# Attention followed by a feed-forward block: the second product by seven half-size block products, one PSUM bank for the first

## The chip, the cores and the metric

The kernel runs on one core of one Trainium2 chip. The metric is the device time of one execution, in microseconds (us). Times given are medians of the runs shown; the profile is of one execution.

## The reference

Attention over 4 batches of 8 heads, 768 tokens, head size 64, in which a query sees the keys of its own hash bucket only; then a feed-forward block with an activation made of softplus and erf. All in float32.

```python
q_bits = (np.einsum('bhsd,dk->bhsk', q, proj) > 0)      # 6 bits; the same for k
mask = q_bucket[:, :, :, None] == k_bucket[:, :, None, :]
scores = np.where(mask, scale * np.matmul(q, k.transpose(0, 1, 3, 2)), -1000000000.0)
attn = softmax(scores)
x = (attn @ v).transpose(0, 2, 1, 3).reshape(3072, 512)
h = x @ w_in                                            # 512 -> 2048
sp = np.maximum(h, 0.0) + np.log1p(np.exp(-np.abs(h)))
out = (h * erf(sp)) @ w_out                             # 2048 -> 512
```

## The kernel before, in words

**Attention** (`attention`) goes over 16 pairs of heads. Scores are computed with the keys on the partitions, ACT takes the exponential straight from PSUM (three slots of two banks), DVE sums the exponentials for the divisor, PE weighs v. Between these, `square_high`, `keep_normal`, `move_bits`, `mask_bits` and `add_rest` turn the weights' float64 bits into float32. The exponential is taken without subtracting a maximum. That is safe while the scores are bounded, so a bound is worked out, and a flag decides at the end whether a general version (`general`) must run too. Before the change the bound comes from the largest magnitudes of q and k: during the feed-forward block `fetch_part` loads q and k once more, 64 pieces, `extremes` takes their maxima on DVE, and `judge` makes the flag.

**The feed-forward block** (`feed_forward`) goes over 6 tiles of 512 tokens (t), each in 4 steps (c); step p = 4 t + c, called a pair in the prediction, treats four of the 16 blocks of 128 hidden features. The first product x @ w_in is done by Strassen's scheme in Winograd's form: `product` computes P1 to P7, seven products of half-size blocks in place of eight, four matmuls of 128x128x256 each. They are summed in three PSUM banks X, Y and Z. `read` (ACT) copies X to the tile h at four stages of its sum, `complete` (DVE) adds Y or Z to three of the four quarters. The sums of x blocks that the scheme needs (`presum_x`) exist twice, one set for each of two x tiles; the sums of w_in are made once in attention.

The activation works on two units of 128 x 1024 a pair: `absolute`, `exponential`, `one_more`, `lost`, `logarithm`, `softplus`, `correct`, `square`, three times `factor` (ACT) and `multiply` (DVE), `saturate`, `gate`. Exp and tanh are in one ACT table, ln in another.

The second product (`project`, L1081) is the plain one: the gated blocks are stationary, w_out streams by, 8 x 2 matmuls of 128x128x512 a pair, 384 in all. They are summed over the four steps in four PSUM banks, one for each 128 tokens; at the end of a tile `store` copies each bank and sends it.

A matmul of float32 operands shows in the trace as two rows of matmul and two of weight load.

**The order** is no order of the source. Every step of both parts is an `Op` with an engine, a cost, a rank, what it comes after, and what buffers it takes and frees. `arrange` plays these through on a model clock and emits each engine's instructions in that order, so every engine then works its list from front to back. On PE the first products rank before the second ones, and h has four buffers, so that the first products run up to four pairs ahead. `late` brings the last pair of heads to its end inside the feed-forward block.

Of the kernel before, what the change touches and what calls it, by code (L numbers as in the profile page):

```python
# [64 lines left out]
S_MAX = 4.0  # L66
# [28 lines left out]
def arrange(ops, rooms):  # L95


    ready = {op.name: None for op in ops}
    names = {op.name: op for op in ops}
    waiting = {}  # L100
    for op in sorted(ops, key=lambda op: op.rank):
        waiting.setdefault(op.engine, []).append(op)
    clock = dict.fromkeys(waiting, 0.0)
    rings = {ring: [] for ring in rooms}
    released = {}
    table = "exp"
    order = []
    while len(order) < len(ops):
        best = None
        for engine, queue in waiting.items():  # L110
            for op in queue:
                start = clock[engine]
                needs = [a for a in op.after if a in names]
                if any(ready[a] is None for a in needs):
                    continue
                for a in needs:
                    away = 0.0 if names[a].engine == engine else names[a].late
                    start = max(start, ready[a] + away)
                if op.take:
                    ring = rings[op.take[0]]  # L120
                    if len(ring) >= rooms[op.take[0]]:
                        end = released.get(ring[-rooms[op.take[0]]])
                        if end is None:
                            continue
                        start = max(start, end)
                if best is None or (start, engine != best[1], op.rank) < (
                    best[0],
                    False,
                    best[2].rank,
                ):  # L130
                    best = start, engine, op
        start, engine, op = best
# [4 lines left out]
        clock[engine] = ready[op.name] = end  # L137
# [4 lines left out]
        waiting[engine].remove(op)  # L142
        order.append(op)
    return order
# [3 lines left out]
def kernel(  # L148
# [34 lines left out]
    norm = ctx.enter_context(tc.tile_pool(name="norm", bufs=1))  # L183
# [14 lines left out]
    most = const.tile([P, 2, B * H], F32, name="most")  # L198
# [58 lines left out]

    def load_x(t):

        x, _ = blocks[t % 2]  # L260
        n = t * T
        while n < (t + 1) * T:
            b, n0 = divmod(n, S)
            m = min(S - n0, (t + 1) * T - n)
            nc.sync.dma_start(
                out=x[:, :, n - t * T : n - t * T + m],
                in_=xs[b][:, :, n0 : n0 + m].rearrange("k p t -> p k t"),
            )
            n += m

    def presum_x(t, k):

        x, ts = blocks[t % 2]
        b11, b12, b21, b22 = x[:, 0:2, 0:TH], x[:, 0:2, TH:T], x[:, 2:4, 0:TH], x[:, 2:4, TH:T]
        t1, t2, t4 = (ts[:, n, :, :] for n in range(3))
        out_, one_, two_ = ((t1, b12, b11), (t2, b22, t1), (b12, b22, b12), (t4, b21, t2))[k]
        nc.vector.tensor_tensor(out=out_, in0=one_, in1=two_, op=ALU.subtract)

    def block_tiles(pool, n):
        x = pool.tile([P, NK, T], F32, name=f"x{n}")  # L280
        ts = pool.tile([P, 3, 2, TH], F32, name=f"ts{n}")
        return x, ts

    blocks.append(block_tiles(const, 0))


# [72 lines left out]
    def attention():  # L359
        NS = NPAIR * 4  # L360
        with (
# [165 lines left out]
            def home(i):  # L527
                return xst if i < NPAIR - 1 else norm
# [14 lines left out]
            def keep_divisor(h):  # L543
                i, half = divmod(h, 2)
                d = pairs[i]
                if half == 0:
                    d["z"] = home(i).tile([P, S], F32, name="z", tag="z")
                nc.scalar.copy(out=d["z"][:, half * HS : (half + 1) * HS], in_=d.pop("z_ps"))

            def leave(h):  # L550
# [4 lines left out]
                if half == 0:  # L555
                    d["x"] = home(i).tile([P, S], F32, name="x", tag="x")
# [44 lines left out]
            def widen(i):  # L601
                d = pairs[i]
                rd = d.pop("rd")
                d["r"] = home(i).tile([P, S], F32, name="r", tag="z")
# [139 lines left out]
            for i in range(NPAIR):  # L744
                n = 4 * i
                if i:
# [6 lines left out]
                        (("weigh", n - 9), ("bits_of", i - 1)),  # L753
# [12 lines left out]
                    )  # L766
                if i == NPAIR - 1:
# [42 lines left out]
            for k in range(4):  # L810
                op(presum_x, (0, k), "DVE", 0.62, (2, 31, 8 + k), (("load_x", 0), ("presum_x", 0, k - 1)))
# [116 lines left out]

    def feed_forward(check, late):
        with (  # L930
            tc.tile_pool(name="xb", bufs=1) as xb,
            tc.tile_pool(name="hp", bufs=4) as hp,
            tc.tile_pool(name="sp", bufs=4) as sp,
            tc.tile_pool(name="work", bufs=2) as work,
            tc.tile_pool(name="outp", bufs=2) as outp,
# [4 lines left out]
            del blocks[1:]  # L940
            blocks.append(block_tiles(xb, 1))
            st = {}

            def product(p, name):
# [3 lines left out]
                x, ts = blocks[t % 2]  # L948
                b11, t3 = x[:, 0:2, 0:TH], x[:, 0:2, TH:T]
                b21, b22 = x[:, 2:4, 0:TH], x[:, 2:4, TH:T]  # L950
                t1, t2, t4 = (ts[:, n, :, :] for n in range(3))
# [3 lines left out]
                into, a, b, first, last = dict(  # L955
                    P1=("X", a11, b11, True, False),
                    P2=("Y", a12, b21, True, True),
                    P3=("Z", s4, b22, False, True),
                    P4=("X", a22, t4, False, True),
                    P5=("Z", s1, t1, True, False),  # L960
                    P6=("X", s2, t2, False, False),
                    P7=("X", s3, t3, False, False),
                )[name]
                if first:
                    tag = into if p != 1 else f"o{'XYZ'.index(into)}"
                    d[into] = ps_f.tile([P, 2, TH], F32, name=into, tag=tag)
                for u in range(2):
                    f = (2 * c + u) * P
                    for kc in range(2):
                        nc.tensor.matmul(  # L970
                            out=d[into][:, u, :],
# [7 lines left out]
            def read(p, q):  # L979

                d = st[p]
                if "h" not in d:
                    d["h"] = hp.tile([P, 2, 4, TH], F32, name="h", tag="h")
                nc.scalar.copy(out=d["h"][:, :, q, :], in_=d["X"])  # L984

            def complete(p, q, which):
                d = st[p]
                h = d["h"][:, :, q, :]
                nc.vector.tensor_tensor(out=h, in0=d[which], in1=h, op=ALU.add)

            def unit(p, u):
                return st[p]["h"][:, u, :, :].rearrange("p q t -> p (q t)")

            def absolute(p, u):
                e = st[p]["e", u] = work.tile([P, 2 * T], F32, name="e", tag="e")
                nc.vector.tensor_scalar(  # L996
                    out=e[:, :].bitcast(I32),
                    in0=unit(p, u).bitcast(I32),
                    scalar1=0x7FFFFFFF,
                    scalar2=None,  # L1000
                    op0=ALU.bitwise_and,
                )

            def exponential(p, u):
                e = st[p]["e", u]
                nc.scalar.activation(out=e, in_=e, func=AF.Exp, scale=-1.0)  # L1006

            def one_more(p, u):
                w = st[p]["w", u] = work.tile([P, 2 * T], F32, name="w", tag="wq", bufs=4)
                nc.scalar.activation(out=w, in_=st[p]["e", u], func=AF.Identity, bias=1.0)  # L1010

            def lost(p, u):

                w = st[p]["w", u]
                nc.vector.scalar_tensor_tensor(  # L1015
                    out=w, in0=w, scalar=-1.0, in1=st[p]["e", u], op0=ALU.add, op1=ALU.subtract
                )

            def logarithm(p, u):
                s = st[p]["s", u] = sp.tile([P, 2 * T], F32, name="s", tag="s")  # L1020
                nc.scalar.activation(out=s, in_=st[p].pop(("e", u)), func=AF.Ln, bias=1.0)  # L1021

            def softplus(p, u):
                s = st[p]["s", u]
                nc.vector.scalar_tensor_tensor(  # L1025
                    out=s, in0=unit(p, u), scalar=0.0, in1=s, op0=ALU.max, op1=ALU.add
                )

            def correct(p, u):
                s = st[p]["s", u]  # L1030
                nc.vector.scalar_tensor_tensor(  # L1031
                    out=s,
                    in0=s,
                    scalar=S_MAX,
                    in1=st[p].pop(("w", u)),
                    op0=ALU.min,
                    op1=ALU.subtract,
                )

            def square(p, u):  # L1040
                z = st[p]["z", u] = work.tile([P, 2 * T], F32, name="z", tag="z")
                nc.scalar.activation(out=z, in_=st[p]["s", u], func=AF.Square)  # L1042

            def factor(p, u, j):
                z = st[p]["z", u]
                if j == 2:
                    q = z
                else:
                    q = work.tile([P, 2 * T], F32, name="q", tag="wq", bufs=4)
                st[p]["q", u, j] = q  # L1050
                nc.scalar.activation(out=q, in_=z, func=AF.Square, bias=cq[:, j : j + 1])  # L1051

            def multiply(p, u, j):
                s = st[p]["s", u]
                nc.vector.scalar_tensor_tensor(  # L1055
                    out=s,
# [364 lines left out]
```

## Time and profile before

| | |
|---|---|
| median of 3 runs | 979.61 us (976.65 to 980.2) |
| the profiled execution | 979.03 us |
| its span, first to last instruction | 976.7 us |
| busy: PE, DVE, ACT | 960.0, 836.3, 733.3 us |
| mean granted PE clock | 1.000 |
| first products of the feed-forward block begin | 345.5 us |
| matmul rows of L1081, of attention's scores (f32) | 768, 768 |

Busy time is the time in which an engine had an instruction in work. Matmuls overlap in the pipeline, so the mean duration of a row is longer than the distance between two rows. Attention fills about the first third of the span, the feed-forward block the rest.

### The profile page before, as it was taken

How to read it: one execution, taken by the hardware profiler on the slowest of the kernel's cores; microseconds unless marked ns; L12 is line 12 of the kernel's file. 1: busy time of each engine (PE TensorE's matmuls, PEld its weight loads, DVE VectorE, ACT ScalarE, POOL GpSimd, SP SyncE). 2: the span in 40 equal slices, each digit the busy share in tenths (PEclk: the TensorE clock that was granted, in tenths of full speed). 3: DMA queues.
4: the chain of work that ended last, by engine and by line, in shares of the span. 5: the costliest groups of instructions: out<-in, count | busy, mean ns of one | idle time of the engine just before them, and what ended most of it. 6: DMA issues, size and time to landing. Idle time of an engine off the chain costs nothing.

```text
span 976.7 us, 11534 instructions
## 1 busy us (share of the span) xinstructions
PE 960.0 (98%) x4297; PEld 559.0 (57%) x4297; DVE 836.3 (86%) x1074; ACT 733.3 (75%) x866; POOL 18.0 (2%) x37
## 2 busy tenths in 40 slices
PE   8999999999999999999999999999999999999997
PEld 3454444444444477666665666666666666666543
DVE  4999998999999928989999999988988899888861
ACT  4775776676676629789889888988698889987970
POOL 0000000000000000000000000000000000000000
PEclk9999999999999999999999999999999999999999
DMA  8455555665455122210121002210220000000001
GB/s 189 114 147 139 135 140 163 151 171 147 127 154 149 56 79 79 92 33 17 54 97 33 32 28 86 71 33 27 65 91 17 1 31 13 1 1 21 23 1 46
DMA packets 61888, 74.55 MB, mean 76 GB/s; under 512 B 33888, under 2 KB 44640, under 8 KB 61824
## 3 DMA queue, kind: packets, MB, share of 16 engines
q1 hardware_dynamic: 56880, 56.75, 21.2%
q0 software_dynamic: 4640, 16.78, 5.5%
q8 instruction: 36, 0.59, 0.3%
q10 hardware_dynamic: 304, 0.20, 0.1%
q14 instruction: 28, 0.23, 0.1%
HBM read 60.92 MB, written 12.78 MB: 75 GB/s over the span
## 4 chain that ended last, share of the span: by engine, by line
PE 92%; DVE 4%; ACT 2%; DMA 1%; issue 0%; SPq 0%; DVEq 0%; ACTq 0%
PE o_ps L1081 32%; PE X L970 16%; PE st L479 15%; PE av L519 12%; PE Z L970 8%; PE Y L970 4%; PE z_ps L536 2%; PE bits L316 2%; DVE s L1055 1%; DMA q<-in_qkT_dram 1%; DVE sum L505 1%; ACT e L493 1%; DVE s L1031 0%; DVE s L1025 0%; DVE most L1109 0%
## 5 line engine op out<-in xcount | busy, mean ns | idle before, releaser
L1081 PE MATMUL o_ps<-w_out_sb,h 128*128 128x512 f32 x768 | 341.4, 592 | 0.0
L1081 PEld LDWEIGHTS o_ps<-w_out_sb,h 128*128 128x128 f32 x768 | 145.8, 190 | 153.0 <-issue 148.0
L493 ACT ACTIVATE e<-st 128x768 f32<-128x768 f32 x192 | 148.9, 818 | 12.7 <-PE st L479 12.6
L479 PE MATMUL st<-q,k 64*128 64x384 f32 x768 | 156.1, 484 | 0.0
L519 PE MATMUL av<-e,v 128*64 128x385 f32 (+1 forms) x768 | 129.5, 486 | 0.0
L505 DVE TENSOR_TENSOR sum<-sum,e 128x768 f32<-128x768 f32 x128 | 121.7, 951 | 7.6 <-ACT e L493 0.7
L1055 DVE SCALAR_TENSOR_TENSOR s<-q,s 128x1024 f32<-128x1024 f32 x96 | 116.3, 1220 | 8.6 <-ACT q L1051 5.5
L1051 ACT ACTIVATE q<-z,cq 128x1024 f32<-128x1024 f32 x96 | 105.8, 1142 | 1.4
L519 PEld LDWEIGHTS av<-e,v 128*64 128x64 f32 x768 | 56.0, 137 | 68.0 <-issue 65.4
L970 PE MATMUL X<-x,w_in_sb 128*128 128x256 f32 x384 | 90.6, 380 | 2.1 <-ACT h L984 1.6
L479 PEld LDWEIGHTS st<-q,k 64*128 64x128 f32 x768 | 68.5, 188 | 33.5 <-issue 33.3
L970 PEld LDWEIGHTS X<-x,w_in_sb 128*128 128x128 f32 x384 | 72.8, 190 | 25.4 <-issue 12.1
L984 ACT COPY h<-X 128x512 f32<-128x512 f32 x96 | 55.2, 575 | 41.7 <-PE X L970 35.6
L557 ACT COPY x<-av 128x384 f32<-128x384 f32 x32 | 15.3, 478 | 92.7 <-PE av L519 74.7
L1015 DVE SCALAR_TENSOR_TENSOR w<-w,e 128x1024 f32<-128x1024 f32 x48 | 58.3, 1221 | 17.7 <-ACT w L1010 17.5
L1025 DVE SCALAR_TENSOR_TENSOR s<-h,s 128x1024 f32<-128x1024 f32 x48 | 58.5, 1220 | 17.1 <-ACT s L1021 17.1
L1042 ACT ACTIVATE z<-s 128x1024 f32<-128x1024 f32 x48 | 50.5, 1052 | 29.0 <-DVE s L1031 28.8
L479 PE MATMUL st<-qb,kb 64*128 64x384 bf16 x384 | 63.8, 325 | 4.1 <-ACT e L493 3.2
L1070 DVE TENSOR_TENSOR h<-h,s 128x1024 f32<-128x1024 f32 x48 | 57.1, 1216 | 3.2 <-ACT s L1066 3.2
L1031 DVE SCALAR_TENSOR_TENSOR s<-s,w 128x1024 f32<-128x1024 f32 x48 | 58.6, 1222 | 1.2
L1006 ACT ACTIVATE e<-e 128x1024 f32<-128x1024 f32 x48 | 50.4, 1050 | 10.6 <-DVE e L996 10.5
L1055 DVE SCALAR_TENSOR_TENSOR s<-z,s 128x1024 f32<-128x1024 f32 x48 | 57.1, 1216 | 0.0
(82 smaller groups left out, 1244.2 us busy)
## 6 DMA issues: line engine op xcount, KB each, us to landing
t<-in_qkT_dram SPq DMA_DIRECT2D x64, 192.0 KB
raw<-in_w_in_dram POOLq DMA_DIRECT2D x16, 512.0 KB, 3.9
raw<-in_w_out_dram POOLq DMA_DIRECT2D x16, 512.0 KB, 3.7
v<-in_v_dram SPq DMA_DIRECT2D x32, 192.0 KB
r<-rd SPq DMA_DIRECT2D x32, 192.0 KB
xs<-x SPq DMA_DIRECT2D x16, 384.0 KB
out_dram<-ob SPq DMA_DIRECT2D x24, 256.0 KB
q<-in_qkT_dram SPq DMA_DIRECT2D x30, 192.0 KB
```

Of the source, the lines that this page charges most:

```text
L479: nc.tensor.matmul(out=st[:, ab, 0:HS], lhsT=d["k" + src][rows, keys], rhs=d["q" + src][rows, cols], start=(part == 0), stop=(part == 1),)
L493: nc.scalar.activation(out=e[:, :, 0:HS], in_=st[:, :, 0:HS], func=AF.Exp, scale=scale)
L505: nc.vector.tensor_tensor(out=d[key], in0=before, in1=block(n, c)[:, :, 0:HS], op=ALU.add)
L519: nc.tensor.matmul(out=d["av"][rows, 0:w], lhsT=d["v"][:, g * GC + c, rows], rhs=e[:, ab, 0:w], start=(g == 0 and c == 0), stop=(g == 1 an ...
L970: nc.tensor.matmul(out=d[into][:, u, :], lhsT=a[:, kc, f : f + P], rhs=b[:, kc, :], start=(first and u == 0 and kc == 0), stop=(last and u ...
L1015: nc.vector.scalar_tensor_tensor(out=w, in0=w, scalar=-1.0, in1=st[p]["e", u], op0=ALU.add, op1=ALU.subtract)
L1025: nc.vector.scalar_tensor_tensor(out=s, in0=unit(p, u), scalar=0.0, in1=s, op0=ALU.max, op1=ALU.add)
L1031: nc.vector.scalar_tensor_tensor(out=s, in0=s, scalar=S_MAX, in1=st[p].pop(("w", u)), op0=ALU.min, op1=ALU.subtract,)
L1051: nc.scalar.activation(out=q, in_=z, func=AF.Square, bias=cq[:, j : j + 1])
L1055: nc.vector.scalar_tensor_tensor(out=s, in0=st[p].pop(("q", u, j)), scalar=ERF_Q[j][1], in1=s, op0=ALU.add, op1=ALU.mult,)
L1070: nc.vector.tensor_tensor(out=h, in0=h, in1=st[p].pop(("s", u)), op=ALU.mult)
L1081: nc.tensor.matmul(out=o_live[tt], lhsT=st[p]["h"][:, u, 2 * fh + half, sub * P : (sub + 1) * P], rhs=w_out_sb[:, fh * NF // 2 + 2 * c + u ...
```

## The change

- **Second product.** The plain product becomes the same seven-product scheme, M1 to M7, on blocks of the gated activations and of w_out, 28 matmuls of 128x128x256 a pair. Each M has a PSUM bank of its own, summed over the four steps of a tile. Sums of gated blocks (`presum_g`, 4 a pair, DVE); sums of w_out (`presum_w`, once for each c, DVE), kept in DRAM (`keep_w`) and loaded again for each later pair (`load_w`, 768 KB, ring of two). At a tile's end `combine` adds the seven banks up, one ACT copy and seven DVE additions, and sends four quarters.
- **First product.** The seven M banks and one bank X are all eight. X takes every first product after the third pair, evicted seven times a pair (4 `read`, 3 `complete`). The first three pairs borrow M banks.
- **Activation.** softplus(h) is computed as ln(1 + exp(min(h, 3.98))) with its correction: `absolute` becomes `clip`, `softplus` is left out. h is held in halves of tokens (8 buffers), e has 4 buffers, w 6.
- **Bound.** `measure` sums the squares of q and k on ACT during attention (64 activations with a summed output); `fetch_part` and `extremes` go. `judge` uses these sums early in the feed-forward block.
- **Buffers.** The sums of x blocks exist once (`x_sum`). The last pair of heads uses the second x tile.
- **Order.** `arrange` takes priorities for each kind of step and a patience of 0.16 us, by which a step of the first rank goes ahead of one that could start that much earlier.

```diff
+PRIORITY = dict(
+    clip=(-0.37, 0.71),
...
+    project=-7.76,
+)
+PATIENCE = 0.16
...
+            start, op = min(
+                (
+                    (start, op)
+                    for start, op in starts
+                    if start <= first + (patience if op.rank[0] == 0 and engine != "PE" else 0.0)
+                ),
+                key=lambda each: (each[1].rank, each[0]),
+            )
...
+            def measure(i, n, half):
+
+                cols = slice(half * HS, (half + 1) * HS)
+                nc.scalar.activation(
+                    out=x_sum[:, 0, :, :].rearrange("p k t -> p (k t)")[:, 0:HS],
+                    in_=pairs[i]["qk"[n]][:, cols],
+                    func=AF.Square,
+                    accum_out=stats[:, n, i, half : half + 1],
+                )
...
-                        (("weigh", n - 9), ("bits_of", i - 1)),
+                        (("weigh", n - 9), ("bits_of", i - 1))
+                        + tuple(("measure", i - 3, m, half) for m in range(2) for half in range(2)),
...
+            def clip(p, v):
+                e = st[p]["e", v] = own("e")
                 nc.vector.tensor_scalar(
+                    out=e, in0=unit(p, v), scalar1=H_MAX, scalar2=None, op0=ALU.min
+                )
...
+            def presum_g(p, k):
...
+                out_, one_, two_, op_ = (
+                    lambda: (d["S", 0], a21, a22, ALU.add),
+                    lambda: (d["S", 1], d["S", 0], a11, ALU.subtract),
+                    lambda: (a21, a11, a21, ALU.subtract),
+                    lambda: (d["S", 3], a12, d["S", 1], ALU.subtract),
+                )[k]()
+                nc.vector.tensor_tensor(out=out_, in0=one_, in1=two_, op=op_)
...
+            def load_w(p):
+                w_sums[p] = wtp.tile([P, 3, 2, TH], F32, name="wt", tag="wt")
+                nc.sync.dma_start(out=w_sums[p], in_=wt_dram[p % NC4])
...
+            def project(p, name, k):
 
                 t, c = divmod(p, NC4)
...
+                a, b = dict(
+                    M1=lambda: (d["h", 0][:, 0, :, :], w_block(c, 0, 0)),
+                    M2=lambda: (d["h", 0][:, 1, :, :], w_block(c, 1, 0)),
+                    M3=lambda: (d["S", 3], w_block(c, 1, 1)),
+                    M4=lambda: (d["h", 1][:, 1, :, :], t4),
+                    M5=lambda: (d["S", 0], t1),
+                    M6=lambda: (d["S", 1], t2),
+                    M7=lambda: (d["h", 1][:, 0, :, :], w_block(c, 0, 1)),
+                )[name]()
...
+                sub, u = divmod(k, 2)
+                nc.tensor.matmul(
+                    out=banks[name][:, sub, :],
+                    lhsT=a[:, u, sub * P : (sub + 1) * P],
+                    rhs=b[:, u, :],
+                    start=(c == 0 and k == 0),
+                    stop=(c == NC4 - 1 and k == 3),
+                    skip_group_check=True,
+                )
...
+            def combine(t, k):
+
+                if k == 0:
+                    outs["u"] = outp.tile([P, 2, TH], F32, name="u", tag="u")
+                    nc.scalar.copy(out=outs["u"], in_=banks["M1"])
                     return
...
+                nc.vector.tensor_tensor(out=outs[into], in0=banks[name], in1=one, op=ALU.add)
...
+            ORDER = ("M1", "M2", "M4", "M5", "M6", "M7", "M3")
...
+                if p < FILL:
+                    x, y, z = (("M1", "M2", "M4"), ("M5", "M6", "M7"), ("M3", "X", "X"))[p]
...
+                else:
+                    steps = (
+                        ("P1", "X", 0, read),
+                        ("P6", "X", 1, read),
+                        ("P7", "X", 3, read),
+                        ("P4", "X", 2, read),
+                        ("P2", "X", 0, complete),
+                        ("P5", "X", 3, complete),
+                        ("P3", "X", 1, complete),
+                    )
...
-            for each in arrange(ops, dict(h=4, e=2, wq=4, s=4, z=2, ob=2)):
+            for each in arrange(ops, dict(h=8, e=4, w=6, wt=2), PATIENCE):
                 each.emit()
```

In `ORDER`, M1 and M2 need the gate of the first token half, M4 that of the second, M5, M6, M7 and M3 the sums S1 to S4 made from both.

More of the change, by code (lines that the diff above doesn't have):

```diff
@@ L104, in arrange @@
+PATIENCE = 0.16
+def arrange(ops, rooms, patience=0.0):
+    names = {op.name: op for op in ops}
+    users, missing = {}, {}
+    for op in ops:
+        needs = {a for a in op.after if a in names}
+        missing[op.name] = len(needs)
+        for a in needs:
+            users.setdefault(a, []).append(op)
+    ranked = sorted(ops, key=lambda op: op.rank)
+    clock = {op.engine: 0.0 for op in ranked}
+    ready, released = {}, {}
     rings = {ring: [] for ring in rooms}
-    released = {}
+    open_ops = {engine: [] for engine in clock}
@@ L106, in arrange, with open_up, start_of @@
     table = "exp"
     order = []
+    def open_up(op):
+        at = 0.0
+        for a in op.after:
+            if a in names:
+                away = 0.0 if names[a].engine == op.engine else names[a].late
+                at = max(at, ready[a] + away)
+        open_ops[op.engine].append((op, at))
+    def start_of(op, at):
+        at = max(at, clock[op.engine])
+        if op.take:
+            ring, room = rings[op.take[0]], rooms[op.take[0]]
+            if len(ring) >= room:
+                at = max(at, released.get(ring[-room], float("inf")))
+        return at
@@ L108, in arrange @@
+    for op in ranked:
+        if not missing[op.name]:
+            open_up(op)
     while len(order) < len(ops):
         best = None
[L110 to L131, printed above, removed]
@@ L132, in arrange @@
-        start, engine, op = best
+        for engine, entries in open_ops.items():
+            starts = [(start_of(op, at), op) for op, at in entries]
+            starts = [each for each in starts if each[0] < float("inf")]
+            if not starts:
+                continue
+            first = min(start for start, _ in starts)
+            start, op = min(
[6 more added lines that the diff above has]
+            )
+            if best is None or start < best[0]:
+                best = start, op
@@ L136, in arrange @@
             end += TABLE_LOAD
-        clock[engine] = ready[op.name] = end
+        clock[op.engine] = ready[op.name] = end
         if op.take:
@@ L141, in arrange @@
             released[what] = end + op.late
-        waiting[engine].remove(op)
+        open_ops[op.engine] = [each for each in open_ops[op.engine] if each[0] is not op]
         order.append(op)
+        for user in users.get(op.name, ()):
+            missing[user.name] -= 1
+            if not missing[user.name]:
+                open_up(user)
     return order
@@ L970, in product @@
                         nc.tensor.matmul(
-                            out=d[into][:, u, :],
+                            out=d[where][:, u, :],
                             lhsT=a[:, kc, f : f + P],
@@ L977, in product, with quarter @@
                         )
-            def read(p, q):
+            def quarter(p, q):
+                fh, th = divmod(q, 2)
                 d = st[p]
[L982 to L989, printed above, removed]
@@ L1008, in one_more, with read @@
[L1008 to L1014, printed above, removed]
+                if ("h", th) not in d:
+                    d["h", th] = hp.tile([P, 2, 2, TH], F32, name="h", tag="h")
+                return d["h", th][:, fh, :, :]
+            def read(p, q, where):
+                nc.scalar.copy(out=quarter(p, q), in_=st[p][where])
@@ new lines, in first_ops @@
+                last_of, seen = {}, set()
+                for k, (name, where, q, fn) in enumerate(steps):
+                    after = (("load", t), ("presum", t, ready.get(name, -1)))
+                    if where in last_of:
+                        after += (last_of[where],)
+                    if where == "X" and chain["X"]:
+                        after += (chain["X"],)
+                    if chain["P"]:
+                        after += (chain["P"],)
+                    op(
+                        (name, p),
+                        "PE",
+                        1.73,
+                        (0, p, k),
+                        product,
+                        (p, name, where, name in ("P1", "P2", "P5"), name in ("P4", "P2", "P3")),
+                        after=after,
+                        late=0.3,
+                    )
+                    chain["P"] = (name, p)
+                    me = (fn.__name__, p, q)
+                    after = ((name, p),)
+                    if fn is complete:
+                        after += (("read", p, q),)
+                    op(
+                        me,
+                        "ACT" if fn is read else "DVE",
+                        0.58 if fn is read else 0.69,
+                        (0, p, k),
+                        fn,
+                        (p, q, where),
+                        after=after,
+                        take=("h", (p, q % 2)) if q % 2 not in seen else None,
+                    )
+                    seen.add(q % 2)
+                    last_of[where] = me
+                    if where == "X":
+                        chain["X"] = me
@@ L1296, in feed_forward @@
                     )
+                op(("check", 0), "PE", 0.3, (0, 1, 9), check, (), after=(("P3", 0), ("late", 0)), late=1.5)
+                for each in ops:
+                    if each.name == ("P2", FILL - 1):
+                        each.after += (("check", 0),)
             else:
```

672 lines of the change are left out of this document (357 added, 315 removed).

## The prediction

> **What bounds the kernel now.** I read the page's busy table first, then the windows cut where the feed-forward (FF) begins, where the last gate ends and at the end, then the chain of waits.
>
> ```profile
> PE 960.0 (98%) x4297; PEld 559.0 (57%) x4297; DVE 836.3 (86%) x1074; ACT 733.3 (75%) x866; POOL 18.0 (2%) x37
> 30.00:345.00 315.00, 310.62 (x2044) 147.00 (x2042) 291.59 (x449) 208.58 (x315) 15.55 (x29) 1.00 0.52 139
> 345.40:363.30 17.90, 17.83 (x82) 14.97 (x83) 4.06 (x7) 3.80 (x8) 0.00 (x0) 1.00 0.26 83
> 363.30:948.40 585.10, 581.65 (x1986) 376.16 (x1985) 520.63 (x563) 504.36 (x523) 0.00 (x0) 1.00 0.12 40
> 948.40:976.70 28.30, 22.87 (x54) 9.84 (x52) 2.76 (x4) 0.00 (x0) 0.00 (x0) 0.99 0.11 40
> PE 92%; DVE 4%; ACT 2%; DMA 1%; issue 0%; SPq 0%; DVEq 0%; ACTq 0%
> 363.99 5.18 PE X L970 x24
> 923.20 48.08 PE o_ps L1081 x112
> 945.95 2.36 DVE L1070 TENSOR_TENSOR h<-h,s 128x1024 f32<-128x1024 f32 x2 [0.66 <-ACT s L1066]
> 971.30 0.69 DVE L1095 COPY ob<-o_ps 128x512 f32<-128x512 f32 x1 [2.74 <-PE o_ps L1081]
> ```
>
> A window row gives start:end, its length, then busy time of PE, weight loads, DVE, ACT, POOL, granted clock. The reader should see a PE that is full in attention and FF at clock 1.00, and a chain that is 92% PE. The last gate ends at 948.3 and PE still has 23.0 us of second products to run, until 971.3 (923.20 + 48.08). DVE is 89.0% busy in the long window (520.63/585.10), ACT 86.2% (504.36/585.10): close seconds.
>
> The two chain rows give the PE's cadence, which the groups' mean durations (pipeline included) do not: a 256-column row costs 5.18/24 = 0.2158 us, a 512-column row 48.08/112 = 0.4293 us. Each f32 matmul of the program is two rows.
>
> **The change part by part.** Groups that are removed or serve as prices (busy, mean ns of one | idle before, releaser):
>
> ```profile
> L1081 PE MATMUL o_ps<-w_out_sb,h 128*128 128x512 f32 x768 | 341.4, 592 | 0.0
> L970 PEld LDWEIGHTS X<-x,w_in_sb 128*128 128x128 f32 x384 | 72.8, 190 | 25.4 <-issue 12.1 <-ACT h L984 3.0 <-ACT x L557 1.2
> L1025 DVE SCALAR_TENSOR_TENSOR s<-h,s 128x1024 f32<-128x1024 f32 x48 | 58.5, 1220 | 17.1 <-ACT s L1021 17.1
> L1109 DVE TENSOR_REDUCE most<-t 128x1 f32<-128x384 f32 x64 | 32.5, 543 | 0.0
> L1095 DVE COPY ob<-o_ps 128x512 f32<-128x512 f32 x24 | 16.5, 686 | 22.0 <-PE o_ps L1081 21.9
> L277 DVE TENSOR_TENSOR ts<-x,ts 128x512 f32<-128x512 f32 x12 | 8.2, 684 | 0.1
> L996 DVE TENSOR_SCALAR e<-h 128x1024 int32<-128x1024 int32 x48 | 31.7, 685 | 0.1
> L984 ACT COPY h<-X 128x512 f32<-128x512 f32 x96 | 55.2, 575 | 41.7 <-PE X L970 35.6 <-PE o_ps L1081 3.8 <-issue 1.7
> L1051 ACT ACTIVATE q<-z,cq 128x1024 f32<-128x1024 f32 x96 | 105.8, 1142 | 1.4
> ```
>
> *Second product on PE.* Out go 768 rows of 512 columns, 768 x 0.4293 = 329.7 us. In come 24 pairs x 7 products x 4 matmuls x 2 = 1344 rows of 256 columns. The first product already runs such rows, with a fresh 128x128 weight load (190 ns) hidden in each 215.8 ns, so 1344 x 0.2158 = 290.1 us. Saved: 39.6 us, all on the path. Half-size rows cost 1.5 us more than half of a full row would (1344 x (0.2158 - 0.4293/2)); that is included.
>
> *DVE in FF.* Out: softplus's maximum 58.5, the extremes 32.5, the stores 16.5, together 107.5. In: four sums of the gated blocks per pair, 96 x 0.684 = 65.7; sums of w_out, 16 x 0.684 = 10.9; combine, 6 tiles x 7 x 0.686 = 28.8; together 105.4. The clip replaces the absolute value, one source of the same shape, so 0.685 again. Net -2.1 us: DVE's work does not fall, while PE's falls by 39.6.
>
> *ACT in FF.* Four reads, twelve activations and the table switches a pair stay; combine adds a copy a tile, 6 x 0.575 = 3.5 us. I take the 48 table loads as unchanged; where the new order needs one more a pair, that is 24 x 1.28 = 31 us more of ACT.
>
> ```profile
> L1021 ACT ACT_TABLE_LOAD x24 | 30.8, 1283 | 0.4
> L1066 ACT ACT_TABLE_LOAD x19 | 24.4, 1283 | 0.3
> L1006 ACT ACT_TABLE_LOAD x5 | 6.4, 1283 | 0.1
> ```
>
> *Does PE stay the bound?* Moved 39.6 us earlier, PE would end at 931.7. Behind the last gate come M4, M5, M6, M7, M3: 40 rows, 8.6 us. So the last gate must end by 923.1, 559.8 us after 363.3. ACT then needs (504.4 + 3.5)/559.8 = 90.7% where 86.2% was seen. DVE: 520.6 - 2.1, less two of the four w_out sums, which fit the idle fill (5.5), and less the last sums and combine, which come after the gate (7.5), is 505.5, or 90.3% where 89.0% was seen. So two ends: PE full, cost 0; or ACT at its old density, 507.9/0.862 = 589.2, last gate at 952.5, PE's end at 952.5 + 8.6 + 0.3 = 961.4, cost 29.7. The rows that choose:
>
> ```profile
> ACT h L984 <- PE X L970: 35.6, 28, 2.9
> ACT z L1042 <- DVE s L1031: 28.8, 20, 2.2
> ACT h L984 <- PE o_ps L1081: 3.8, 5, 1.0
> DVE w L1015 <- ACT w L1010: 17.5, 24, 1.6
> ```
>
> (Waits inside FF: total, times, longest.) Of ACT's 80.7 us of idle time in the window, 39.4 are reads that wait for a full PE: ACT's old density was partly PE's pace. Without those it is 504.4/(585.1 - 39.4) = 92.4%, above what is needed. The rest is ACT and DVE waiting for each other, which more buffers in flight (four e, six w) ease and do not abolish. I stand nearer to the first end: +7.
>
> *One bank X for all seven first products after the third pair.* Each must be evicted before the next starts; PE runs second products meanwhile. PE, then ACT, from the timeline:
>
> ```profile
> 599.99 1.89 PE L970 MATMUL X<-ts,w_sum 128*128 128x256 f32 x8
> 601.72 1.88 PE L1081 MATMUL o_ps<-w_out_sb,h 128*128 128x512 f32 x4
> 603.44 1.89 PE L970 MATMUL X<-x,w_in_sb 128*128 128x256 f32 x8
> 602.09 0.57 ACT L984 COPY h<-X 128x512 f32<-128x512 f32 x1
> 624.30 0.58 ACT L984 COPY h<-X 128x512 f32<-128x512 f32 x1 [0.16 <-PE o_ps L1081]
> ```
>
> The product is over at 601.88, read from 602.09 to 602.66, and the next X product starts at 603.44: one second product, 1.72 us, covers an eviction that needs 0.21 + 0.57. After the change there are seven evictions and seven second products (12.1 us) a pair, exactly one each, with about 0.9 us over for ACT or DVE to finish the instruction they are in (1.14 or 1.22 at most, about half on average). Cost 0 while second products are at hand; if not, 0.8 to 2 us a product. The row at 624.30 shows a read held until a second product freed its h buffer: P runs four pairs ahead, and that stays.
>
> *Attention.* 64 squares on ACT. Nearest rows:
>
> ```profile
> L557 ACT COPY x<-av 128x384 f32<-128x384 f32 x32 | 15.3, 478 | 92.7 <-PE av L519 74.7 <-DMA xs<-x 11.8 <-PE st L479 3.5
> L403 ACT ACTIVATE keep<-raw 128x512 f32<-128x512 f32 x32 | 22.1, 690 | 4.1 <-DVE top L439 4.1
> PE st L479 <- ACT e L493: 3.2, 3, 1.2
> raw<-in_w_out_dram POOLq DMA_DIRECT2D x16, 512.0 KB, 3.7
> ```
>
> No row shows an activation that also sums; I bound it by 0.478 and 0.690, 31 to 44 us in all. ACT is idle for 106.4 of the 315 us, the larger part some 2.9 us at a time ahead of a `leave` (92.7/32), so they fit. If one stands in front of an exponential, scores wait for the PSUM slot: at the mean of the wait row, 1.07 us, 64 of them would cost 68 us. Ends 0 and 68; the idle row is nearer, and I take +1. Each next fetch of q, k, v now waits on SP for the squares of three pairs before; the row sums' transfers of earlier pairs stand behind it on SP, and the hash product of the next pair waits for it. It costs nothing while the squares are done a pair later.
>
> *Transfers.* 64 fetches of 192 KB leave FF. Four stores and twenty loads of 768 KB for the w_out sums come; by the 512 KB row an estimate of 5.6 us each, and each has about a pair's time (24 us) between the buffer coming free and its use at M4. Cost 0; 5 us a pair if that cover went. On SP the loads of x and the output stand behind them.
>
> *Single x sums.* At five tile borders two DVE sums (1.4 us) stand between the old P5 and the new P6, covered by P3, P1 and second products; inside the +7.
>
> *Tail and rest.* After M7 three combines (2.1 us) run beside M3 (1.7), then the last combine and its transfer, behind two others sent just before: +1, ends 0 and 2. The bound's check moves from mid-FF into the fill, where DVE is idle: 0.
>
> Sum against the profiled execution: 976.7 - 39.6 + 7 + 1 + 1 = 946.1 us of span. It took 979.03 us with 2.3 around the span, so 948.4; the median of the three runs lies 0.6 higher: 949.
>
> **The rivals.**
> 1. *The vector engines keep their pace.* ACT at 86.2%: cost 29.7 in place of 7, so 972. For it: the ACT-DVE waits above. Against it: the 39.4 us of reads waiting for PE.
> 2. *The one bank stalls PE, slower.* PE stands still at X because evictions answer late or second products are missing. 21 pairs x 7 = 147 products. If each eviction first waits for a whole instruction of 1.14 us, the gap is 0.21 + 1.14 + 0.57 + 0.26 (the restart) = 2.18 against 1.73 of cover: 0.45 x 147 = 66, from a floor of 942 to 1008. It decides from 0.29 us a product on (42/147). For it: DVE and ACT would both be near 91%. Against it: the read at 602.09, 0.2 us after its product's end. The 0.26 is the first product after a wait, 1.99 against 1.73:
>
> ```profile
> 345.47 1.99 PE X L970 x8
> 347.46 1.73 PE Y L970 x8
> ```
>
> The Trainium skill, "Perfetto Trace Analysis", section "Optimizing Tensor Performance", says that independent matmul groups should rotate through different PSUM banks so that an eviction overlaps the next group's matmuls; by it the old X, Y, Z are right and one X is a step back, and the time is this rival's. The trace bears it out only where nothing else stands ready for PE. The same section says that larger matmuls are more efficient; the two chain rows agree, with the 1.5 us above.
>
> 3. *PE gains less than counted*, because weight loads of the gated blocks show: 190 of 215.8 ns is close. If every row cost 0.245 the gain would be gone (979). Against it: the 24 rows at 363.99 with the same loads.
>
> **How the numbers follow.** Near-full PE, 938 to 960: 0.62. Pace kept, 960 to 975: 0.20. No net change, within 0.5% (what a measurement here can tell from none, 4.9 us): 0.06. Rival 2: 0.07. The squares' bad end: 0.03. Rival 3 is in the 0.06. Below 938: 0.02. The low end is the floor 976.7 - 39.6 + 1 + 1 + 2.9 = 942, less 4 of the 6 us in which PE ran no row in FF before (625.8 us from 345.5 to 971.3, against 329.7 + 290.1 of rows). The high end is rival 1. Faster 0.84, same 0.06, slower 0.10.
>
> **What would show it.** Rows of the second product 1344 at 0.216 cadence; FF's DVE busy time within 5 us of before and ACT's within 8; PE idle in FF of 5 to 12 us; the last gate some 9 to 15 us before PE's end. Rival 1 shows as PE waiting at second products for DVE with ACT-DVE waits unchanged, rival 2 as many PE waits of X for ACT and DVE reads. I am wrong if attention's end moves beyond 350, if the table loads exceed 48, or if PE's idle time in FF is above 30 us.

## The result, and the profile after

The changed kernel takes 938.06 us (median of 4 runs, 937.16 to 941.07); the kernel before, with a run added on the same chip, 979.83. The ratio is 0.9586, with a 95% interval of 0.9556 to 0.9615: 41.8 us less. The forecast was 949, with a range of 938 to 972, so the time lies at the range's lower edge: 0.06 us inside, with two of the four runs below it. The profiled execution is the slowest of the four, 941.07 us with a span of 939.2.

From the page after, the windows cut at the same places as before (attention; from 363.3 to the end of the last gate), and three rows of the chain of waits (start, length, what):

```profile
PE 921.9 (98%) x4875; PEld 666.6 (71%) x4875; DVE 835.4 (89%) x1093; ACT 779.0 (83%) x1004; POOL 18.5 (2%) x37
30.00:345.00 315.00, 312.00 (x2062) 146.32 (x2058) 294.77 (x452) 247.94 (x438) 16.37 (x30) 1.00 0.52 139
363.30:921.30 558.00, 556.00 (x2573) 487.35 (x2572) 506.77 (x564) 508.42 (x530) 0.00 (x0) 1.00 0.16 52
PE 92%; DVE 4%; DMA 2%; ACT 1%; issue 0%; SPq 0%; ACTq 0%; DVEq 0%
346.02 7.17 PE M L1044 x32
895.79 33.68 PE M L1184 x156
```

PE is as full as before (98%), at the same clock, and still 92% of the chain. A row of the second product costs 33.68/156 = 0.2159 us, the price that the first product had. ACT and DVE are now 91.1% and 90.8% busy in the long window, where they were 86.2% and 89.0%.

The ends of the feed-forward (FF), from the timeline after:

```profile
920.02 1.23 DVE L1126 TENSOR_TENSOR h<-h,e 128x1024 f32<-128x1024 f32 x1 [1.12 <-ACT e L1122]
929.29 1.89 PE L1184 MATMUL M<-w_out_sb,S 128*128 128x256 f32 x8
931.55 0.68 DVE L1213 TENSOR_TENSOR v<-M,v 128x512 f32<-128x512 f32 x1
932.26 1.58 SPq L1216 DMA_DIRECT2D out_dram<-v  x1
```

The last gate ends at 921.3, 27 us earlier than before. PE issues its last product from 929.29 to 931.0. So FF takes PE 585.0 us (346.0 to 931.0) where it took 625.8: 580.2 of the two products' rows and 4.8 beside them, against 619.8 and 6.0. The span's 37.5 us less are 39.6 of rows and 1.2 of gaps, less 0.55 in attention and 2.8 at the end (931.0 to 939.2, where it was 971.3 to 976.7).

What PE waited for in FF (total, times, longest):

```profile
PE X L1044 <- ACT h L1062: 1.6, 3, 0.7
PE M L1044 <- ACT x L613: 0.6, 1, 0.6
PE M L1184 <- DVE h L1126: 0.4, 1, 0.4
```

The one bank X holds PE up for 1.6 us in all, missing gates for 0.4. ACT, in turn, waits less for PE's products than before (35.6 us, in the prediction's lines):

```profile
ACT h L1062 <- PE X L1044: 22.6, 28, 2.7
```

ACT's waits for DVE in FF shrink as well: those that the profile lists add up to 24.5 us, where they were 43.4.

How X is covered, from the timeline (PE, then DVE):

```profile
621.51 1.89 PE L1044 MATMUL X<-x,w_in_sb 128*128 128x256 f32 x8
623.24 0.59 PE L1184 MATMUL M<-w_out_sb,h 128*128 128x256 f32 x2
623.67 1.03 PE L1184 MATMUL M<-w_out_sb,S 128*128 128x256 f32 x4
624.54 1.89 PE L1044 MATMUL X<-x_sum,w_sum 128*128 128x256 f32 x8
623.44 0.69 DVE L1066 TENSOR_TENSOR h<-X,h 128x512 f32<-128x512 f32 x1
```

A product ends at 623.40, `complete` starts 0.04 us later, and six rows of second products fill the 1.30 us until X is used again.

### The profile page after: what moved, and what is told of

It is laid out like the page before. It is cut to its first block, busy times and chain, and to the rows that moved or that the text cites. A ratio compares the mean times of both kernels' runs of the same rounds, so it can differ in the third digit from the quotient of the medians.

```text
span 939.2 us, 12854 instructions
## 1 busy us (share of the span) xinstructions
PE 921.9 (98%) x4875; PEld 666.6 (71%) x4875; DVE 835.4 (89%) x1093; ACT 779.0 (83%) x1004; POOL 18.5 (2%) x37
## 4 chain that ended last, share of the span: by engine, by line
PE 92%; DVE 4%; DMA 2%; ACT 1%; issue 0%; SPq 0%; ACTq 0%; DVEq 0%
PE M L1184 30%; PE X L1044 27%; PE st L521 15%; PE av L561 12%; PE M L1044 3%; PE bits L358 2%; PE z_ps L592 2%; DVE sum L547 1%; DMA k<-in_qkT_dram 1%; DMA zd<-z 0%; DVE e L1098 0%; ACT e L535 0%; DMA zc<-zd 0%; DVE top L481 0%; DVE w_sum L691 0%
## 5 line engine op out<-in xcount | busy, mean ns | idle before, releaser
L1111 DVE SCALAR_TENSOR_TENSOR e<-w,e 128x1024 f32<-128x1024 f32 x144 | 173.9, 1220 | 9.2 <-ACT w L1107 6.5
L1107 ACT ACTIVATE w<-w,cq 128x1024 f32<-128x1024 f32 x144 | 160.2, 1143 | 1.5
L1184 PE MATMUL M<-w_out_sb,h 128*128 128x256 f32 x576 | 140.2, 379 | 0.4 <-DVE h L1126 0.4
L1184 PEld LDWEIGHTS M<-w_out_sb,h 128*128 128x128 f32 x576 | 109.4, 190 | 15.6 <-DVE h L1126 0.8
L1184 PE MATMUL M<-wt,S 128*128 128x256 f32 x384 | 92.5, 379 | 0.0
L1044 PE MATMUL X<-x_sum,w_sum 128*128 128x256 f32 x344 | 81.7, 380 | 1.6 <-ACT h L1062 1.6
L1184 PEld LDWEIGHTS M<-wt,S 128*128 128x128 f32 x384 | 72.9, 190 | 10.0
L1044 PEld LDWEIGHTS X<-x_sum,w_sum 128*128 128x128 f32 x344 | 65.0, 190 | 11.9 <-ACT h L1062 3.2
L1126 DVE TENSOR_TENSOR h<-h,e 128x1024 f32<-128x1024 f32 x48 | 58.1, 1220 | 7.1 <-ACT e L1122 6.9
L1098 DVE TENSOR_TENSOR e<-e,w 128x1024 f32<-128x1024 f32 x48 | 57.9, 1219 | 4.6 <-ACT e L1094 4.6
```

The lines of the kernel that those rows point to most:

```text
L1044: nc.tensor.matmul(out=d[where][:, u, :], lhsT=a[:, kc, f : f + P], rhs=b[:, kc, :], start=(first and u == 0 and kc == 0), stop=(last and ...
L1098: nc.vector.tensor_tensor(out=s, in0=s, in1=st[p].pop(("w", v)), op=ALU.subtract)
L1111: nc.vector.scalar_tensor_tensor(out=s, in0=st[p].pop(("q", v, j)), scalar=ERF_Q[j][1], in1=s, op0=ALU.add, op1=ALU.mult,)
L1126: nc.vector.tensor_tensor(out=h, in0=h, in1=st[p].pop(("s", v)), op=ALU.mult)
L1184: nc.tensor.matmul(out=banks[name][:, sub, :], lhsT=a[:, u, sub * P : (sub + 1) * P], rhs=b[:, u, :], start=(c == 0 and k == 0), stop=(c = ...
```

## The experiments

Theory A: PE's rows are the bound before and after, and the saved rows come through whole. Rivals: ACT and DVE are at a limit of their own in the one kernel or the other (B), the tuned order is what makes the saving possible (C), or some smaller part of the change costs or gains.

Several of these kernels leave out or repeat work and compute something else; they serve for their times only. They ran on three chips, on which the kernel before took 978.1 to 979.5 us, where the 938.06 belongs to 979.83. With this and the spread of one kernel's runs, a difference between two runs below is uncertain by some 3 us.

**1. A little less second product.** In `project`:

```diff
+                if name == "M3" and k in (1, 2):
+                    return
```

> The changed kernel without two of the four matmuls of M3 in each pair (part of the second product is left out; the order of all else on every engine stays). PE loses 24 x 2 x 2 rows x 0.2158 = 20.7 us. Theory A, PE alone sets the pace and ACT and DVE, 90% busy, have room: 917 to 922 us. Theory B, at 90% in this order ACT and DVE are at their limit as well: 933 to 938 us.

Measured: 928.83 us (926.94 to 930.87). Of 20.7 us taken from PE, 9.2 came through: between A and B. In this run PE waits at X:

```profile
PE X L1044 <- ACT h L1062: 3.4, 4, 1.2
PE X L1044 <- DVE h L1066: 2.7, 8, 0.4
PEld X L1044 <- DVE h L1066: 8.7, 16, 0.8
910.29 1.22 DVE L1126 TENSOR_TENSOR h<-h,e 128x1024 f32<-128x1024 f32 x1 [1.12 <-ACT e L1122]
```

The weight loads of first products wait for `complete` 16 times, which is missing in the list of the changed kernel, and the last gate comes only 9.7 us earlier. With experiment 2: PE is the bound of the changed kernel, but ACT, DVE and the evictions of X, in this order, stand some 9 us behind it.

**2. A little more second product.** The mirror: those two matmuls are issued twice (their part of M3 counts double).

```diff
+                for again_ in range(2 if name == "M3" and k in (1, 2) else 1):
```

> The changed kernel with two of the four matmuls of M3 in each pair run twice (order unchanged): 20.7 us more on PE, the mirror of the run with two of them left out, which gave back 9.2 us. Theory A, PE sets the pace: all of it comes through, 957 to 960 us. Theory F, part of PE's time in the feed-forward is cover for waits of ACT and DVE and so not all on the path: 945 to 954 us.

Measured: 958.89 us (958.42 to 959.93), 20.8 more for 20.7 us of rows: theory A; theory F falls. PE's waits of X are the same 1.6 us as without the addition.

**3. Half the second product: where is the limit of ACT and DVE?**

```diff
+                if k in (1, 2):
+                    return
```

> The changed kernel without two of the four matmuls of each of M1 to M7 (half of the second product is left out; order unchanged): 145 us less on PE, so that ACT and DVE must set the time. It shows where their own limit lies. Theory A: DVE's 525 us of FF at 95% density instead of 90%, 553 + 13 for the fill + 9 for the end, some 10 to 25 us below the changed kernel: 913 to 928 us, and no more than that since the order was made for a slower PE. Theory B: 930 to 938 us.

Measured: 909.53 us (908.80 to 910.44), 28.5 below the changed kernel, a little under the range of A. The long window up to this run's last gate, and PE's waits:

```profile
363.30:892.50 529.20, 455.69 (x1905) 354.75 (x1903) 500.93 (x559) 501.99 (x526) 0.00 (x0) 0.98 0.16 54
PE X L1044 <- ACT h L1062: 42.0, 60, 3.1
PE X L1044 <- DVE h L1066: 20.9, 43, 1.5
```

With PE out of the way ACT and DVE come to 94.9% and 94.7%: the limit of this order, 29 us off. PE now stands at X for 62.9 us in 103 waits. That is what the prediction's second rival would look like, but it does not price the one bank: with 145 us less to do, PE has to wait somewhere, and half of the cover is gone at the same time. A kernel with a second bank for the first products was not run; the seven M banks and X are all there are.

**4. The same for the kernel before.**

```diff
-                for fh in range(2):
+                for fh in range(1):
```

> The kernel before with half of its second product left out (one of the two matmuls of each project step; order unchanged): 165 us less on PE. It shows what ACT and DVE could do before. Theory A, their old density (86% and 89%) was PE's pace: they run up to 92 to 95%, the last gate comes 25 to 40 us earlier and the time is 925 to 950 us. Theory B (rival 1 of the prediction), it was their own pace: the last gate stays at 948 and only the tail of second products shrinks, 962 to 972 us.

Measured: 954.71 us (953.02 to 955.74), between the two theories.

```profile
363.30:937.50 574.20, 480.48 (x1644) 325.88 (x1642) 520.31 (x565) 502.88 (x523) 0.00 (x0) 0.93 0.13 40
PE X L970 <- ACT h L984: 81.7, 41, 4.7
ACT h L984 <- PE X L970: 27.6, 22, 2.9
```

With half of its second product gone, the old order brings its last gate from 948.3 to 937.5, ACT to no more than 87.6% and DVE to 90.6%. (PE's granted clock was 0.93 in this window, so its rows were slower and the relief is less than the 165 us counted.) ACT's reads still wait 27.6 of their 35.6 us for X, though PE is no longer full. A PE that ends at 931.7 needs the last gate by 923.1. So the old order, with the old work on ACT and DVE, would not have kept up with the new PE time. How far it would have come with the changed kernel's work on DVE, no run shows.

**5. The order without its priorities.** All entries of `PRIORITY` are 0; the rest of `arrange`, the buffers and the work are those of the changed kernel.

```diff
-    clip=(-0.37, 0.71),
+    clip=(0.0, 0.0),
...
-    project=-7.76,
+    project=0.0,
```

> The changed kernel with all priorities of the steps set to 0 (the patience stays), so that within the second rank the older pair goes first. Theory A, the buffers alone keep PE full: 937 to 945 us. Theory C, the tuned priorities are what brings ACT and DVE to 90% with PE full: 955 to 985 us, with PE waiting at second products for gates.

Measured: 962.63 us (961.62 to 963.02), 24.6 above the changed kernel: theory C.

```profile
363.30:942.90 579.60, 561.16 (x2570) 487.88 (x2569) 508.16 (x563) 514.50 (x538) 0.00 (x0) 0.99 0.15 50
PE M L1184 <- DVE h L1126: 14.6, 6, 10.7
922.84 5.58 PE L1184 MATMUL M<-w_out_sb,h 128*128 128x256 f32 x16 [10.73 <-DVE h L1126]
941.69 1.23 DVE L1126 TENSOR_TENSOR h<-h,e 128x1024 f32<-128x1024 f32 x1 [1.12 <-ACT e L1122]
```

ACT and DVE reach 88.8% and 87.7%, the last gate ends at 942.9, and PE stands 14.6 us before second products whose gates are missing, 10.73 of them at once, where the changed kernel loses 0.4 us to that in all. DVE's work in the window is within 1.4 us of the changed kernel's (508.16 against 506.77); for DVE only when it is done differs. ACT has 6.1 us more (514.50 against 508.42), for the plain order switches its tables 60 times in FF instead of 52. Of the 41.8 us, 24.6 hang on the order, by the measure of this plain one. The saved rows are the source, the order lets them through.

**6. Fewer buffers.** Two for e and four for w, with an order made anew by the same priorities.

```diff
-            for each in arrange(ops, dict(h=8, e=4, w=6, wt=2), PATIENCE):
+            for each in arrange(ops, dict(h=8, e=2, w=4, wt=2), PATIENCE):
```

> The changed kernel with two buffers for e and four for w in place of four and six; the order is made anew for them with the same priorities. Theory A'', the buffers in flight are what lets ACT and DVE run at 91% with PE full: 960 to 990 us. Theory C, the priorities do it and two units in flight are enough: 938 to 948 us.

Measured: 1035.64 us (1032.09 to 1037.16), slower than before the change and beyond the range of A''. The groups show one reason that was not expected, the table loads (first this run, then the changed kernel):

```profile
L1094 ACT ACT_TABLE_LOAD x47 | 60.3, 1283 | 0.8
L1079 ACT ACT_TABLE_LOAD x35 | 44.9, 1283 | 3.4 <-DVE e L1073 3.0
L1122 ACT ACT_TABLE_LOAD x12 | 15.4, 1283 | 0.2
```

```profile
L1094 ACT ACT_TABLE_LOAD x26 | 33.4, 1283 | 0.5
L1079 ACT ACT_TABLE_LOAD x15 | 19.2, 1283 | 0.3
L1122 ACT ACT_TABLE_LOAD x11 | 14.1, 1283 | 0.2
```

There are 94 loads instead of 52, 54 us more on ACT. The likely reason is that with two units in flight the two units of a pair can hardly share a switch between exp and ln; no run tests that alone. For the rest of the 98 us, DVE's waits for ACT in FF add up to 111 us, where they were 22. The priorities were found for other buffers, and how much of this is theirs was not separated.

**7. DVE's saved work.** The change dropped softplus's maximum (58.5 us) and the extremes (32.5). This puts one instruction a pair back, in `correct`:

```diff
+                if v == 0:
+                    nc.vector.scalar_tensor_tensor(
+                        out=s, in0=s, scalar=-1.0e30, in1=s, op0=ALU.max, op1=ALU.min
+                    )
```

> The changed kernel with one more DVE instruction of 128x1024 behind correct in one of the two units of a pair (it leaves the values as they are; order unchanged): 24 x 1.22 = 29 us more on DVE, about what the extremes took. It prices the work that the change took off DVE. Theory A', DVE's 54 us of idle time in the feed-forward takes most of it up: 938 to 946 us. Theory B', the slack is only the 9 us by which time fell when M3 was halved, and the rest comes through: 953 to 962 us.

Measured: 951.91 us (951.03 to 952.32), 13.9 more for 29 us of work: between the two, nearer to B'. DVE goes to 93.6% (533.17/569.60), the last gate to 932.9:

```profile
363.30:932.90 569.60, 560.33 (x2572) 485.11 (x2570) 533.17 (x587) 507.45 (x529) 0.00 (x0) 1.00 0.15 50
ACT w L1106 <- DVE e L1100: 21.4, 18, 2.2
```

About half is taken up by idle time, half comes through. But the instruction stands in the middle of a unit's chain, where softplus's maximum stood, and the second row shows ACT waiting 21.4 us for it (L1100). So part of the price may be the longer chain and not DVE's time; an extra instruction outside the chain was not tried. Either way DVE's work is not a side matter after the change: what is taken off it pays for the sums that the second product's scheme adds.

**8. The extremes, taken from the kernel before.**

```diff
-        feed_forward(judge, late)
+        nc.vector.memset(flag, 0)
+        feed_forward(None, late)
```

> The kernel before without the second loading of q and k and their maxima in the feed-forward (the flag is set to 0 by a memset; no bound is worked out): 32.5 us less on DVE, 64 fetches less. One part of the change alone. Theory A, PE set the pace: 977 to 980 us, no difference. Theory B, DVE and ACT set it: 955 to 970 us.

Measured: 978.12 us (974.71 to 979.25) beside 978.11 for the kernel before; ratio 0.9994 (0.9980 to 1.0007). Theory A. DVE has 27.7 us less in the window (492.90 for 520.63), and PE runs as before (the window is that of the kernel before; in this run the last gate ended at 945.2 already):

```profile
363.30:948.40 585.10, 583.01 (x1983) 375.88 (x1982) 492.90 (x492) 502.28 (x523) 0.00 (x0) 1.00 0.05 18
```

Work of DVE outside the chain is worth nothing before the change. Experiment 7 prices work inside the chain after it, so the two are not the same measure.

**9. The squares in attention.**

```diff
-                            measure,
...
+    nc.vector.memset(stats, 1.0)
```

> The changed kernel without the 64 squares on ACT in attention (the bound's sums are set to 1 by one memset; the bound is then no bound of this input). In the trace of the change they add 39.8 us to ACT's busy time in attention, and the feed-forward begins 0.55 us later than before. Theory A, they lie in ACT's gaps: 937 to 938.5 us, no difference that can be measured. Theory D, they push exponentials back and cost PE time: 931 to 935 us.

Measured: 940.96 us (938.73 to 941.25), ratio to the kernel before 0.9616 (0.9600 to 0.9632) beside 0.9586 (0.9556 to 0.9615) with them: nothing gained; theory D falls. The time lies above theory A's range too; why was not found, and the two profiled executions have the same span, 939.2. Without the squares FF begins at 345.60, with them at 346.02. PE's waits for exponentials in attention are the same, first without the squares, then with them:

```profile
PE st L522 <- ACT e L536: 2.4, 2, 1.2
```

```profile
PE st L521 <- ACT e L535: 2.4, 2, 1.2
```

What a square with a sum costs, from the groups of the changed kernel:

```profile
L579 ACT ACTIVATE x_sum<-q 128x384 f32<-128x384 f32 x32 | 16.9, 529 | 0.4
L579 ACT ACTIVATION_READ_ACCUMULATOR x_sum<-q 128x1 f32 x32 | 6.4, 201 | 0.0
```

**10. The last transfers on two queues.**

```diff
-                    nc.sync.dma_start(
+                    queue = nc.scalar if t == NTILE - 1 and k in (5, 7) else nc.sync
+                    queue.dma_start(
```

> The changed kernel with two of the last tile's four outputs (the second c and v) sent from ACT's queue instead of SP's. The span goes on for 8.2 us behind the last second product where it was 5.4 before, and the last send sits 1.58 us on SP. Theory A, the sends stand in line on SP's queue: 1 to 2 us less, 936 to 937 us. Theory E, the transfers themselves or what follows them take the time: 937.5 to 938.5 us.

Measured: 937.71 us (936.03 to 939.63), ratio 0.9586 (0.9568 to 0.9603), the same as without. In its profile the last send takes 0.38 us to issue instead of 1.58, and the span ends 6.7 us behind the last product (930.9 to 937.6) instead of 8.2:

```profile
929.21 1.89 PE L1184 MATMUL M<-w_out_sb,S 128*128 128x256 f32 x8
932.18 0.38 ACTq L1217 DMA_DIRECT2D out_dram<-v  x1
```

So the last send does stand in line on SP's queue, as A has it, but the time falls into E's range, and a gain of 1 us is below what the runs can tell from none.

## Why the prediction was right, point by point, and where it was off

- *The saved rows, 39.6 us.* Right: 0.2159 us a row, 37.5 us in the span, and experiment 2 shows rows on the path one to one.
- *The work of ACT and DVE.* Right: 505.5 and 507.9 us were worked out for the long window, 506.77 and 508.42 measured. The table loads went from 48 to 52 in FF. The prediction had named more than 48 as a sign that it is wrong; the four cost 5.1 us of ACT (4 x 1.283), and ACT still met the deadline.
- *The deadline.* Right: the last gate had to end by 923.1 with PE full, and it ended at 921.3.
- *The stalls, +7.* This is the term that was mis-sized: PE's idle time in FF fell by 1.2 us, to 4.8, just under the 5 to 12 that were forecast. Its argument was weak as well. It took the reads that wait for a full PE as a sign that ACT's 86.2% was PE's pace, and credited more buffers in flight with the rest. Experiment 4 shows that the old order reaches 87.6% with PE relieved, and that 27.6 us of the reads' waits stay, so the pace was mostly its own. Nor are there more buffers: e and w are 10 tiles, where e, wq, s and z were 2 + 4 + 4 + 2 = 12. What let PE run full are the priorities, to which the prediction gave no part: with the same buffers and none of them, PE waits 14.6 us for gates (experiment 5). So PE staying the bound was forecast rightly, but in part on a wrong ground.
- *Rival 1, 972.* Did not come. Without the priorities the time lies between the forecast and this rival: 962.63 in experiment 5, with PE waiting for gates, as the rival said.
- *Rival 2, one bank.* 1.6 us. The cover of one second product for one eviction was the right price. By the rule of the Trainium skill, "Perfetto Trace Analysis", section "Optimizing Tensor Performance", groups should rotate through banks. Here one bank is enough, with matmuls of other banks ready in between: 1.30 us of them in the stretch shown, against an eviction of 0.04 + 0.69. How little of this cover would do was not separated (experiment 3).
- *Rival 3.* No sign of it: 0.2159.
- *Attention, +1.* 0.55 in the profile, and no gain without the squares. The 0.55 itself says little: in the profiles of kernels with the very same attention, FF begins anywhere from 343.7 (experiment 3) to 346.0. The upper bound of 0.690 for one square was too low: with the read-out, an instruction of its own, it is 0.529 + 0.201 = 0.730.
- *Tail, +1.* 2.8: three transfers of 256 KB within 1.4 us, of which the last waited on SP's queue.
- *From 949 to 938.* On the profiled execution the forecast was 948.4 against 941.07: 8.2 from the stalls, 0.45 from attention and 0.5 around the span, less 1.8 of the tail. The other 3.6 are the offset to the median: the profiled execution was 0.6 below the median before and is 3.0 above it now. What makes these runs differ by 3 us stayed open; as the beginnings of FF differ by up to 2.3 us, a part of it arises in attention. That the median still falls into the range, by 0.06 us, is luck; the prediction gave a time below 938 a chance of 0.02.

## What to carry to other kernels

When the bound engine is relieved, work out the density that the next engines need to keep up, over the stretch from their first to their last instruction; cutting the bound engine's work out for a test shows what they can reach (here ACT 87.6% with the old order, 94.9% with the new, 91% needed). A gain on one engine can hang on the order of the others, so change the two together and test them apart. Work taken off an engine that is not the bound was worth nothing here before the change (experiment 8); once the bound had moved up to that engine, work added to it cost about half of itself (experiment 7).

## What the runs showed that was not expected

An activation with a summed output is two instructions: 0.53 us for 128x384 and 0.19 to 0.20 for reading the sum. Halving the buffers of the activation chain nearly doubled the loads of ACT's tables (52 to 94, 1.283 us each). A wait of PE cost more than it lasted: behind the 10.73 us in experiment 5 the granted clock was 0.65 from 922.8 to 928.3, and 16 rows took 5.58 us, where 16 rows of the second product otherwise show as 3.62. And 20.7 us of PE work, added in 2 and taken away in 1, came through as 20.8 and 9.2: a kernel can sit so near the meeting point of two bounds that only one direction shows the first.
